# A fused attention and feed-forward kernel: states transposed by one DMA, a bank for the second G1, copies spread over two engines, and a G2 step moved

## The chip, the cores and the metric

The kernel runs on one core of one Trainium2 chip. The metric is the device time of one execution in microseconds (us). A "run" is one execution; medians over runs are given. The profile is one execution taken by the hardware profiler; its span (first to last instruction) is about 1.8 us shorter than the time of the same execution.

Engines are named as the profile names them: PE is TensorE's matmuls, PEld its weight loads, DVE is VectorE, ACT is ScalarE, POOL is GpSimd, SP is SyncE (here the queue that issues stores and DMA transposes). PSUM is the memory that matmuls write to, used here as eight banks; SBUF is the memory that holds their operands. A table load is the instruction with which ACT changes from exp to SILU or back; it takes 1.28 us in these traces.

## The reference

```python
# x: (8, 8, 512, 64), state: (8, 8, 32, 64); B, H, S, D and 32 state rows
a     = softmax(x @ state^T / 8);  xread = a  @ state      # 512 rows per batch
a2    = softmax(state @ x^T / 8);  sread = a2 @ x          # 32 rows per batch
t     = concat(xread, sread) over rows, heads side by side # (4352, 512)
h     = t @ w_in                                           # 512 -> 2048
out   = (h * sigmoid(h)) @ w_out                           # 2048 -> 512
```

The kernel never forms xread. For each batch it multiplies the states into w_in first (it calls the product W), so that h is the normalised a times W.

## The kernel before

Words used below:

- **G1 k** is one step of the first big product: 128 of the 2048 hidden columns, all 512 tokens of a batch. It is two matmuls of 512 columns into one PSUM bank, followed by one SILU on ACT that writes `g`. Steps 0 to 15 belong to batch 0, 16 to 31 to batch 1.
- **G2(b, tt, ft)** is one matmul of the second product: 128 tokens (tt), hidden block ft, summed over 16 blocks in one bank.
- **aT** is the normalised a, transposed so that G1 can read it.
- **W matmuls** are groups of eight small matmuls that form a piece of W, which DVE or ACT then copies to SBUF.

The pool that G1 writes to (`psH`) has two banks, so G1 k+2 has to wait for the SILU of G1 k. All eight PSUM banks are in use: `psO` has two (o0, o1), `psH` two (h1), `psA` four (a0 to a3).

```python
def g1_first():                                   # G1 0, in two halves, two banks
    ...
    for hg in range(2):
        for i in range(2):
            nc.tensor.matmul(pss[i][:, 0:256], W1[0][:, hg, 0:128], aT[0][:, hg, ds(2*i, 2), :],
                             start=(hg == 0), stop=(hg == 1), ...)
    for i in range(2):
        nc.scalar.activation(g[:, ds(256*i, 256)], pss[i][:, 0:256], func=SILU, bias=0.0)

def g1_half(k, hg):
    if hg == 0:
        h_ps[k] = psH.tile([128, 512], FP32, tag="h1", name="h1")
    ...

def G2(b, tt, ft):
    if ft == 0:
        if b == 0 and tt >= 2:
            outs[tt] = psA.tile([128, DM], FP32, tag=f"a{tt - 2}", name="o_a")   # tt 3 uses a1
    ...

# --- start, batch 0
pe_transpose_x(0, 1, 2, new_h, (nc.vector, nc.vector))
...
norm(0, 1, ((nc.vector, 0, 4),))
pss0 = w1_mms(0, [(0, 128)])
nc.scalar.activation(warm[:], busy[:, 0:1], func=SILU, bias=0.0)   # table load for SILU
w1_out(0, [(0, 128)], (nc.scalar, nc.scalar), pss0)
...
pe_transpose_a(0, 0, nc.scalar, new_o)
for c in (0, 2):
    pe_transpose_a(0, 1, nc.vector, (new_o, bank)[c // 2], c, 2)
upto(1)                                                            # G1 0
w1_out(0, [(128, 128)], (nc.vector, nc.vector), pss0)
w1_out(0, [(128, 256)], both, pss0, 128)

# --- end of batch 0 (G2 of the last 128 tokens), G1 of batch 1 begins
for ft in range(F3, NFT):
    ...
    if ft == 14:
        ...
        pss1 = w1_mms(1, cols, tail_bank)
        w1_out(1, cols, both, pss1)          # both = (DVE, ACT)
        ...
        transpose_x(2)                       # DMA transpose on SP
    if ft == 15:
        upto(NFT + 2)                        # G1 16, G1 17
    G2(0, 3, ft)
upto(NFT + 3)                                # G1 18
store(0, 3, nc.vector)

# --- batch 1
            if tt == 0:
                upto(NFT * b + min(lead + ft, NFT))        # lead is 4 for batch 1
            if b == 1:
                if at == (0, 1):
                    transpose_x(3)
                    transpose_state()        # eight PE transposes into a bank
                    for u in range(2):
                        evict_state(u, nc.vector)
```

The softmax here doesn't subtract the row's maximum and nothing guards it: scores larger than these inputs give would overflow.

## Time and profile before

| | before |
|---|---|
| time, median of the 3 runs known at the prediction | 217.85 us (217.42 to 218.06) |
| profiled run | 217.45 us, span 215.7 us |
| PE busy | 208.4 us, 97% of the span |

The page of the kernel before, its first lines (engine, busy us, share of the span, instructions):

```profile
span 215.7 us, 3904 instructions
PE 208.4 (97%) x1583; PEld 97.1 (45%) x1583; DVE 75.6 (35%) x167; ACT 140.2 (65%) x245; POOL 39.5 (18%) x61
```

PE is busy nearly all the time, so the time changes only when a PE instruction or a PE gap goes away. The list of waits of PE in the same kernel, cut (who waited for whom: us in total, times, longest):

```profile
PE ps_w L463 <- DVE W L158: 0.7, 1, 0.7
PE h L516 <- ACT g L510: 0.4, 1, 0.4
...
PE h L516 <- ACT g L548: 0.3, 1, 0.3
```

The list has only waits that leave the pipeline idle for over 0.15 us. Smaller losses are found by stepping through the starts. A 512-column matmul in an unbroken row starts 0.216 us after the one before. The Trainium skill ("TensorE: Matmul & The Clock Gate", section "Wait — 56ns, not 53.3ns?") states 215.7 ns for this, and the trace agrees. Every start that comes later than that is a loss, and "wait" below means the excess over 0.216 us.

The start in the timeline of PE, kernel before (start us, us, engine, line, operation, out<-in, shape, count, and in brackets the idle time and who ended it). L501 is G1 0, L516 the other G1, L557 a G2:

```profile
11.65 0.60 PE L501 MATMUL h<-aT,W 128*128 128x256 bf16 x4
12.61 0.59 PE L516 MATMUL h<-aT,W 128*128 128x512 bf16 x2 [0.36 <-ACT g L510]
13.04 0.59 PE L557 MATMUL o<-w_out_sb,g 128*128 128x512 bf16 x2
13.47 0.59 PE L557 MATMUL o_a<-w_out_sb,g 128*128 128x512 bf16 x2
```

G1 1 starts 0.96 us after G1 0 began. It waits for the first SILU of G1 0, because it takes that SILU's bank.

The place where batch 1 begins, PE and then ACT, kernel before (L463 are W matmuls, L278 the state transposes):

```profile
37.98 0.62 PE L463 MATMUL ps_w<-w_in_sb,stT 64*32 64x512 bf16 x16
38.54 0.39 PE L557 MATMUL o_a<-w_out_sb,g 128*128 128x512 bf16 x1
38.76 1.03 PE L516 MATMUL h<-aT,W 128*128 128x512 bf16 x4
39.63 0.38 PE L557 MATMUL o_a<-w_out_sb,g 128*128 128x512 bf16 x1
40.11 1.08 PE L516 MATMUL h<-aT,W 128*128 128x512 bf16 x4
41.03 0.38 PE L557 MATMUL o<-w_out_sb,g 128*128 128x512 bf16 x1
41.39 0.59 PE L516 MATMUL h<-aT,W 128*128 128x512 bf16 x2
41.82 0.61 PE L278 MATMUL ps_st<-ident,st_b 128*128 128x128 bf16 x8
42.27 0.38 PE L557 MATMUL o<-w_out_sb,g 128*128 128x512 bf16 x1
```

```profile
38.49 1.08 ACT L156 ACTIVATE W<-ps_w 128x512 bf16<-128x512 f32 x2 [0.77 <-PE ps_w L463]
39.46 1.09 ACT L548 ACTIVATE g<-h 128x512 bf16<-128x512 f32 x2
```

The G2 at 39.63 should be followed 0.216 us later by G1 18, but G1 18 starts at 40.11: a wait of 0.27 us. It waits for the SILU of G1 16. That SILU starts only at 39.46, because ACT copies two pieces of W first. Two smaller waits follow, 0.06 us before G1 19 and 0.14 us before G1 20. The eight state transposes hold PE from 41.82 to 42.27.

### The profile page before, as it was taken

The numbers are of one execution on the slowest core, as the hardware profiler recorded it, in microseconds if no ns is written. First come the engines' busy times: TensorE is split into PE (matmuls) and PEld (weight loads), VectorE is DVE, ScalarE is ACT, GpSimd is POOL, SyncE is SP. The second block draws the span as 40 slices with busy tenths as digits, with TensorE's granted clock in tenths as the row PEclk, the third lists the DMA queues.
The fourth block names the chain that finished last, engine by engine and source line by source line (L and its number), as shares of the span: only waits on it lengthen the run. The fifth ranks groups of instructions, "written<-read, shape, count | busy, mean of one in ns | idle before, by whom it ended". The sixth has DMA issues, their size and how long they took to land.

```text
span 215.7 us, 3904 instructions
## 1 busy us (share of the span) xinstructions
PE 208.4 (97%) x1583; PEld 97.1 (45%) x1583; DVE 75.6 (35%) x167; ACT 140.2 (65%) x245; POOL 39.5 (18%) x61
## 2 busy tenths in 40 slices
PE   7889999999899999999999999999999999999993
PEld 2443345445344444444444444444444444466653
DVE  3724237654961056106610552135411415200011
ACT  3766578699656985699559957786665366634410
POOL 8583013701520122004010402000200000000000
PEclk9999999999999999999999999999999999999999
DMA  6999999792339567273637194114310211011112
GB/s 197 195 204 206 294 273 331 194 272 101 77 95 256 176 105 195 62 233 96 157 97 232 68 184 112 49 49 106 86 59 6 101 49 52 0 50 49 52 49 97
DMA packets 41858, 28.40 MB, mean 132 GB/s; under 512 B 26992, under 2 KB 36720, under 8 KB 41840
## 3 DMA queue, kind: packets, MB, share of 16 engines
q1 hardware_dynamic: 35664, 20.39, 34.6%
q0 software_dynamic: 5888, 7.64, 17.1%
q8 instruction: 12, 0.20, 0.4%
q10 hardware_dynamic: 288, 0.13, 0.2%
q14 instruction: 6, 0.05, 0.1%
HBM read 17.43 MB, written 8.91 MB: 122 GB/s over the span
## 4 chain that ended last, share of the span: by engine, by line
PE 86%; DVE 5%; ACT 4%; DMA 2%; issue 1%; POOL 0%; POOLq 0%
PE o L557 46%; PE h L516 25%; PE ps_w L463 4%; PE h L537 3%; DMA x_f<-in_x_dram 2%; PE o_a L557 2%; PE o_part L579 2%; DVE W L158 2%; DVE rs L379 1%; ACT exp_nat L320 1%; PE ps_sr L415 1%; DVE rc L431 1%; PE ps_xt L251 1%; ACT g L548 1%; ACT W L156 1%
## 5 line engine op out<-in xcount | busy, mean ns | idle before, releaser
L557 PE MATMUL o<-w_out_sb,g 128*128 128x512 bf16 x496 | 132.2, 379 | 0.0
L548 ACT ACTIVATE g<-h 128x512 bf16<-128x512 f32 (+1 forms) x143 | 81.5, 573 | 35.8 <-PE h L516 21.8
L557 PEld LDWEIGHTS <-g 128*128 128x128 bf16 x528 | 50.0, 98 | 58.0 <-issue 3.6
L516 PE MATMUL h<-aT,W 128*128 128x512 bf16 x254 | 74.8, 379 | 0.8 <-ACT g L510 0.4
L158 DVE COPY o_sb<-o 128x512 f32<-128x512 f32 x15 | 10.4, 691 | 90.2 <-PE o L557 85.5
L516 PEld LDWEIGHTS <-W 128*128 128x128 bf16 x254 | 24.6, 98 | 31.7 <-DVE W L158 2.0
L158 DVE CAST W<-ps_w 128x512 bf16<-128x512 f32 (+2 forms) x34 | 21.5, 653 | 25.8 <-PE ps_w L463 25.8
L156 ACT ACTIVATE W<-ps_w 128x512 bf16<-128x512 f32 (+2 forms) x34 | 17.9, 567 | 13.3 <-PE ps_w L463 13.3
L158 POOL CAST x_nat<-x_f 128x512 bf16<-128x512 f32 x24 | 14.6, 653 | 33.2 <-DMA x_f<-in_x_dram 22.2
L156 ACT ACTIVATE o_sb<-o 128x512 f32<-128x512 f32 x16 | 9.6, 597 | 12.1 <-PE o L557 8.9
L362 POOL TENSOR_TENSOR an<-e,rcn 128x512 bf16<-128x512 bf16 x5 | 7.6, 1518 | 49.5 <-DVE rcn L360 49.5
L463 PE MATMUL ps_w<-w_in_sb,stT 64*32 64x512 bf16 (+2 forms) x264 | 11.1, 375 | 0.7 <-DVE W L158 0.7
L557 PE MATMUL o_a<-w_out_sb,g 128*128 128x512 bf16 x32 | 10.2, 379 | 0.0
L537 PE MATMUL h<-xmT,w_in_sb 128*128 128x256 bf16 x64 | 9.6, 273 | 0.0
L537 PEld LDWEIGHTS <-w_in_sb 128*128 128x128 bf16 x64 | 6.3, 98 | 3.9
L164 PE MATMUL ps_busy<-busy 128*128 128x512 bf16 x16 | 6.0, 491 | 1.2 <-DVE warm L171 1.2
L463 PEld LDWEIGHTS <-stT 64*32 64x32 bf16 x264 | 3.4, 89 | 7.3 <-issue 4.9
L382 POOL TENSOR_TENSOR an<-exp_nat,rc 128x512 bf16<-128x512 bf16 x3 | 3.1, 1050 | 19.2 <-ACT eT L346 11.4
L749 ACT ACT_TABLE_LOAD x5 | 6.4, 1283 | 0.1
L346 ACT ACTIVATE eT<-ps_scT 128x512 bf16<-128x512 f32 x10 | 5.4, 595 | 1.6 <-PE ps_scT L332 1.6
L359 DVE TENSOR_REDUCE rs<-e 128x32 f32<-128x1024 bf16 x5 | 6.0, 1208 | 0.0
L108 POOL DMA_DIRECT2D x_f<-in_x_dram x4 | 3.3, 842 | 12.1 <-DVE x_rows L158 10.0
(76 smaller groups left out, 105.1 us busy)
## 6 DMA issues: line engine op xcount, KB each, us to landing
out_dram<-o_sb SPq DMA_DIRECT2D x33, 256.0 KB, 2.4
x_f<-in_x_dram SPq DMA_DIRECT2D x4, 1024.0 KB, 6.2
x_f<-in_x_dram POOLq DMA_DIRECT2D x2, 1024.0 KB, 12.6
w_in_sb<-in_moe_w_in_dram POOLq DMA_DIRECT2D x3, 512.0 KB, 9.6
w_out_sb<-in_moe_w_out_dram POOLq DMA_DIRECT2D x3, 512.0 KB, 11.3
x_f<-in_x_dram SPq DMA_DIRECT2D x2, 512.0 KB, 4.7
x_f<-in_x_dram POOLq DMA_DIRECT2D x2, 512.0 KB, 14.3
w_out_sb<-in_moe_w_out_dram POOLq DMA_DIRECT2D x2, 256.0 KB, 7.7
```

The costliest lines, as they stand in the source:

```text
L156: nc.scalar.activation(dst, src, func=COPY, bias=0.0)
L158: eng.tensor_copy(dst, src)
L164: nc.tensor.matmul(ps[:], busy[:, 0:128], busy[:], start=True, stop=True, skip_group_check=True)
L346: nc.scalar.activation(t[:, hg], scT_ps[hg][:], func=EXP, bias=0.0, scale=SCALE)
L359: nc.vector.tensor_reduce(rs[:], e2[b][:], axis=AX, op=ADD)
L362: eng.tensor_tensor(a[:, hg], e2[b][:, hg], rc[:, hg].to_broadcast([128, 4, 4, NS]), op=MULT)
L463: nc.tensor.matmul(pss[f, hg][ds(32 * s, 32), 0:n], stT[ds(r, 64), b, h // 2, s % 2, :], w_in_sb[ds(r, 64), h // 2, ds(f, n)], start=True, ...
L516: nc.tensor.matmul(h_ps[k][:], W1[b][:, hg, ds(128 * ft, 128)], aT[b][:, hg, :, :], start=(hg == 0), stop=(hg == 1), skip_group_check=True,)
L537: nc.tensor.matmul(ps[:, 0:256], w_in_sb[:, kt, ds(128 * ft, 128)], xmT[:, :, kt].rearrange("p t n b -> p t (n b)"), start=(kt == 0), stop ...
L548: nc.scalar.activation(g[:, 0:n], ps[:, 0:n], func=SILU, bias=0.0)
L557: nc.tensor.matmul(outs[tt][:], gt[b * NFT + ft][:, ds(128 * tt, 128)], w_out_sb[:, ft, :], start=(ft == 0), stop=(ft == NFT - 1), skip_gr ...
L749: nc.scalar.activation(warm[:], busy[:, 0:1], func=SILU, bias=0.0)
```

## The change

Its intent: shorten the start, take the state transposes off PE, and remove the waits where batch 1 begins. The diff, complete except for the definition lines that are cut as marked:

```diff
-    st_ps = []
-    def transpose_state():
-        ps = bank([128, 8, B, 4, 2, 2], BF16, "ps_st")
-        ... eight nc.tensor.transpose(..., st_b[:, m, :], ident[:])
+    st_x = pers.tile([128, 8, B, 4, 2, 2], BF16)
+    def transpose_states():
+        nc.sync.dma_start_transpose(
+            st_x.rearrange("q m b k u n -> q m (b k u n)"), st_b.rearrange("p m w -> p (m w)")
+        )
@@ evict_state
-                    st_ps[0][
+                    st_x[
@@ g1_first
-        for hg in range(2):
-            for i in range(2):
+        for i in range(2):
+            for hg in range(2):
@@ g1_half
-            h_ps[k] = psH.tile([128, 512], FP32, tag="h1", name="h1")
+            pool, tag = (psA, "a1") if k == 1 else (psH, "h1")
+            h_ps[k] = pool.tile([128, 512], FP32, tag=tag, name="h1")
@@ start
-    pe_transpose_x(0, 1, 2, new_h, (nc.vector, nc.vector))
+    pe_transpose_x(0, 1, 2, new_h, (nc.vector, nc.scalar))
-    norm(0, 1, ((nc.vector, 0, 4),))
+    norm(0, 1, ((nc.vector, 0, 4),), 2)
-    pe_transpose_a(0, 0, nc.scalar, new_o)
     for c in (0, 2):
-        pe_transpose_a(0, 1, nc.vector, (new_o, bank)[c // 2], c, 2)
+        pe_transpose_a(0, 0, nc.scalar, new_o, c, 2)
+    for c in (0, 2):
+        pe_transpose_a(0, 1, nc.vector, bank, c, 2)
     upto(1)
     w1_out(0, [(128, 128)], (nc.vector, nc.vector), pss0)
-    w1_out(0, [(128, 256)], both, pss0, 128)
+    w1_out(0, [(128, 256)], (nc.vector, nc.vector), pss0, 128)
+    upto(2)
@@ end of batch 0
-            w1_out(1, cols, both, pss1)
+            w1_out(1, cols, (nc.vector, nc.vector), pss1)
             ...
+            transpose_states()
             transpose_x(2)
-        if ft == 15:
             upto(NFT + 2)
         G2(0, 3, ft)
@@ batch 1
                         transpose_x(3)
-                        transpose_state()
+                    if at == (0, 4):
                         for u in range(2):
                             evict_state(u, nc.vector)
-                    if at == (0, 4):
                         spread_x(2)
```

Called "the start part" below: everything in `g1_first`, `g1_half` and "start". Called "the batch 1 part": the rest.

More of the change, by code (lines that the diff above doesn't have):

```diff
@@ L270 @@
     pe_transpose_x(0, 0, 2, new_o, (nc.vector, nc.vector))
-    st_ps = []
-    def transpose_state():
-        ps = bank([128, 8, B, 4, 2, 2], BF16, "ps_st")
-        st_ps.append(ps)
-        for m in range(8):
-            nc.tensor.transpose(
-                ps[:, m].rearrange("p b k u n -> p (b k u n)"), st_b[:, m, :], ident[:]
-            )
+    st_x = pers.tile([128, 8, B, 4, 2, 2], BF16)
[3 more added lines that the diff above has]
+        )
     def evict_state(u, eng):
```

## The prediction

> **What bounds the kernel now.** TensorE. The profile page gives PE busy 208.4 us of a 215.7 us span (97%), clock granted in full. From start to start a 512-column matmul takes 0.216 us in the timeline; the Trainium skill ("TensorE: Matmul & The Clock Gate", "Wait — 56ns, not 53.3ns?") states 215.7 ns warm, so the trace agrees. Only a TensorE instruction or gap removed can count. From 62 us on the timeline has almost no longer step (45 to 93 ns each). The gaps lie in the start, in batch 0, and where batch 1 begins.
>
> **Start (to 13.9 us).** The chain of waits runs x load, exp, a 1.28 us table load, ACT W copies, ACT copy of aT (to 11.60), first G1 (11.65), SILU (12.17), then G1 of step 1 at 12.605, held by the SILU for its bank: 0.52 us more than the natural step. The change
> - splits the ACT aT copy: its first half (estimate 0.39 us, as another 256-column ACT copy) is ready at 11.43 instead of 11.60; the first SILU then needs two matmuls instead of three: it starts at 11.9 instead of 12.17;
> - gives G1 of step 1 its own bank: it starts at about 12.0, held by its DVE copies of W instead of the SILU, and the first G2 starts at about 12.45 instead of 13.035;
> - but that bank (a1) is the one that the fourth G2 accumulates in, so this G2 waits for the SILU of step 1 (0.60 us, ending near 13.2). I expect it at 13.26, against 13.68.
>
> Net gain at the second G1/G2 step: 0.42 us. The ACT copy of x and the split reduction gain nothing, since ACT's chain ends last.
>
> Batch 0 keeps it if the weights are there: each load lands 1.1 us or more before its use (second w_in block lands 14.6, used 15.72; third 20.0, used 21.34), though the queue is saturated there and won't move. Its gaps (0.2 to 0.4 us at 21.3, 22.6, 28.1, 29.4) are tied to PE's own progress and shift along.
>
> **Start of batch 1 (37.9 to 42.5 us).** Eight state transposes on PE (41.820 to 42.266): 0.446 us removed. In their place one DMA transpose on the SP queue: 8 blocks; the e<-eT transposes of the same size take 1.3 us of the queue and 3.1 us to land, so it lands near 42.5 and the DVE copies end near 45.5. First need: the batch 2 scores at 49.4. The x transposes behind it are delayed 1.3 us, with over 2 us to spare. Off the path.
> The gaps at 40.11 (0.27), 40.60 (0.06) and 41.39 (0.14 us) come from ACT evicting W (2 x 0.54 us) ahead of the SILUs. With W all on DVE and a G2 (0.216 us) between G1 17 and G1 18 they shrink to about 0.03 + 0.14. Gain about 0.28 us.
> Together 0.73 us; the 0.68 us wait at 58.94 (DVE chain of batch 1) stays.
>
> **Predicted.** 217.85 - 0.42 - 0.73 = 216.7 us; 8 in 10 between 216.2 and 217.4. Faster by over 2%: 1%; within 2%: 98%; slower: 1%.
>
> **Right if** the after trace shows: G1 step 1 starting within 0.4 us of the first G1's end; a short wait before the fourth G2; no state transposes on PE; G1 18 without a wait; the second G2 step of batch 1 (42.27 before) near 41.1; everything behind shifted by the same 1.1 us.
>
> **Wrong if** halves of a tile are not tracked apart (start gain only 0.2); DVE, with four W copies and the state copies, becomes late for a G1 or the scores; the DMA transpose lands after about 46 us; or a weight load lands later and absorbs the start's gain.

## The result, and the profile after

| | before | after |
|---|---|---|
| time, median of 4 runs | 217.64 us (217.42 to 218.06) | 216.30 us (216.27 to 216.76) |
| ratio | | 0.9941 (95% interval 0.9919 to 0.9963) |
| profiled run | 217.45 us, span 215.7 us | 216.30 us, span 214.5 us |

A ratio is the mean time of one kernel's fast runs over that of the other's of the same rounds, so it is not quite the ratio of the medians quoted beside it.

The page and the list of PE's waits (cut likewise), kernel after:

```profile
span 214.5 us, 3893 instructions
PE 208.0 (97%) x1575; PEld 96.8 (45%) x1575; DVE 76.7 (36%) x170; ACT 139.5 (65%) x244; POOL 39.4 (18%) x61
```

```profile
PE ps_w L460 <- DVE W L158: 0.7, 1, 0.7
...
PE h L514 <- ACT g L546: 0.3, 1, 0.3
PE ps_at L396 <- ACT W L156: 0.2, 1, 0.2
```

Eight matmuls are gone, the wait for the SILU of G1 0 is gone, the 0.7 us wait of batch 1 stayed, and a new wait is there: a transpose of a (`ps_at`) waits for ACT's copy of W. The same code has other line numbers than before (L514 was L516, L555 was L557, L460 was L463, L498 was L501).

The start in PE's timeline, kernel after:

```profile
11.41 0.70 PE L498 MATMUL h<-aT,W 128*128 128x256 bf16 x4
12.03 0.60 PE L514 MATMUL h<-aT,W 128*128 128x512 bf16 x2
12.47 0.59 PE L555 MATMUL o<-w_out_sb,g 128*128 128x512 bf16 x2
12.90 0.79 PE L555 MATMUL o_a<-w_out_sb,g 128*128 128x512 bf16 x2
13.53 0.59 PE L514 MATMUL h<-aT,W 128*128 128x512 bf16 x2
```

G1 1 now follows G1 0 by 0.61 us instead of 0.96. The two `o_a` matmuls take 0.79 us together instead of 0.59: the second, at 13.318, waits 0.20 us. It writes bank a1, which the SILU of G1 1 reads until 13.267.

The place where batch 1 begins, PE and then ACT, kernel after:

```profile
38.16 1.04 PE L514 MATMUL h<-aT,W 128*128 128x512 bf16 x4
39.04 0.59 PE L555 MATMUL o_a<-w_out_sb,g 128*128 128x512 bf16 x2
39.47 1.07 PE L514 MATMUL h<-aT,W 128*128 128x512 bf16 x4
40.37 0.38 PE L555 MATMUL o<-w_out_sb,g 128*128 128x512 bf16 x1
40.75 0.59 PE L514 MATMUL h<-aT,W 128*128 128x512 bf16 x2
41.18 0.38 PE L555 MATMUL o<-w_out_sb,g 128*128 128x512 bf16 x1
```

```profile
38.81 1.08 ACT L546 ACTIVATE g<-h 128x512 bf16<-128x512 f32 x2 [1.46 <-PE h L514]
40.10 1.08 ACT L546 ACTIVATE g<-h 128x512 bf16<-128x512 f32 x2 [0.21 <-PE h L514]
```

The SILU of G1 16 starts 0.64 us after G1 16 now (before: 0.70), but G1 18 comes one G2 later in PE's order, and it starts at 39.47 without a wait. Waits of 0.04 us (before G1 19) and 0.16 us (before G1 20) remain. The G2 that stood at 42.27 stands at 41.18.

What became of the states is in the view of the new tile, kernel after:

```profile
L158 DVE COPY stT<-st_x x8: 320/324/335, 42.5 to 44.9; 64x192 bf16<-64x192 bf16 x8
L275 SPq DMA_TRANSPOSE st_x<-st_b x1: 1402/1402/1402, 39.1 to 39.1; - x1
...
DMA to landing us min/median/max: 3.3/3.3/3.3
```

The DMA transpose occupies the SP queue for 1.40 us and lands 3.3 us after its issue, at 42.45. The copies end at 45.19 and the first matmul that needs them starts at 48.30. The x transposes behind it landed at 44.49 and 47.25 (before 43.45 and 46.21), the first of them also needed at 48.30.

### Where the time went, by stretches

Single executions differ at the start (see the experiments), so the trace was cut at four marks on PE and ACT and the stretches compared. T is the start of ACT's table load ahead of the first SILU. The first W mark is the first W matmul of batch 0's column 512, near 15.7 us. The column-score mark is the first matmul of batch 3's scores, near 52 us, in which states are the rows (`ps_scT`). The numbers are starts in the traces, in us:

| kernel | T | T to first W | first W to column scores | column scores to end |
|---|---|---|---|---|
| before | 9.207 | 6.510 | 36.390 | 163.573 |
| after | 9.260 | 6.091 | 35.669 | 163.500 |
| difference | +0.053 | -0.419 | -0.721 | -0.073 |

The sum is -1.16 us, the difference of the two spans. The stretches, not the spans, are compared below.

T itself comes 0.053 us later after the change. The last copy of the transposed x ended at 8.420 us on DVE before; it ends at 8.475 on ACT now, and the scores behind it start at 8.531 instead of 8.478. e_bound, with the start of before, has T at 9.210; the four runs below with the new start, no late x load and the first transposes not cold throughout have it at 9.264 to 9.274.

The last 0.073 us lie wholly behind PE's work: from the column scores to the last matmul all starts, counted from that mark, agree within 0.01 us in the two traces, and from the start of the last matmul to the end of the span it takes 3.526 us after and 3.600 before.

### The profile page after: what moved, and what is told of

The parts are those of the page before. It is cut to its first block, busy times and chain, and to the rows that moved or that the text cites. A ratio compares the mean times of both kernels' runs of the same rounds, so it can differ in the third digit from the quotient of the medians.

```text
span 214.5 us, 3893 instructions
## 1 busy us (share of the span) xinstructions
PE 208.0 (97%) x1575; PEld 96.8 (45%) x1575; DVE 76.7 (36%) x170; ACT 139.5 (65%) x244; POOL 39.4 (18%) x61
## 4 chain that ended last, share of the span: by engine, by line
PE 87%; DVE 4%; POOL 3%; ACT 3%; issue 1%; POOLq 0%
PE o L555 47%; PE h L514 26%; PE ps_w L460 4%; PE h L535 3%; PE o_a L555 2%; PE o_part L577 2%; DVE W L158 1%; POOL w_in_sb L149 1%; POOL w_out_sb L152 1%; ACT exp_nat L317 1%; DVE rs L376 1%; PE ps_sr L412 1%; DVE rc L428 1%; PE ps_xt L251 1%; PE ps_scT L329 1%
## 5 line engine op out<-in xcount | busy, mean ns | idle before, releaser
L555 PE MATMUL o<-w_out_sb,g 128*128 128x512 bf16 x496 | 132.2, 379 | 0.0
L555 PEld LDWEIGHTS <-g 128*128 128x128 bf16 x528 | 50.0, 98 | 57.6 <-issue 3.2
L514 PE MATMUL h<-aT,W 128*128 128x512 bf16 x254 | 74.8, 379 | 0.4 <-ACT g L546 0.3
L514 PEld LDWEIGHTS <-W 128*128 128x128 bf16 x254 | 24.5, 98 | 31.8 <-issue 2.0
L158 DVE CAST W<-ps_w 128x512 bf16<-128x512 f32 (+2 forms) x37 | 23.0, 649 | 25.3 <-PE ps_w L460 25.3
L156 ACT ACTIVATE W<-ps_w 128x512 bf16<-128x512 f32 (+1 forms) x31 | 16.4, 570 | 12.6 <-PE ps_w L460 12.6
L460 PE MATMUL ps_w<-w_in_sb,stT 64*32 64x512 bf16 (+2 forms) x264 | 11.1, 375 | 0.7 <-DVE W L158 0.7
L555 PE MATMUL o_a<-w_out_sb,g 128*128 128x512 bf16 x32 | 10.2, 379 | 0.0
L460 PEld LDWEIGHTS <-stT 64*32 64x32 bf16 x264 | 3.4, 89 | 7.3 <-issue 4.9
L748 ACT ACT_TABLE_LOAD x5 | 6.4, 1283 | 0.1
```

The costliest lines, as they stand in the source:

```text
L156: nc.scalar.activation(dst, src, func=COPY, bias=0.0)
L158: eng.tensor_copy(dst, src)
L460: nc.tensor.matmul(pss[f, hg][ds(32 * s, 32), 0:n], stT[ds(r, 64), b, h // 2, s % 2, :], w_in_sb[ds(r, 64), h // 2, ds(f, n)], start=True, ...
L514: nc.tensor.matmul(h_ps[k][:], W1[b][:, hg, ds(128 * ft, 128)], aT[b][:, hg, :, :], start=(hg == 0), stop=(hg == 1), skip_group_check=True,)
L555: nc.tensor.matmul(outs[tt][:], gt[b * NFT + ft][:, ds(128 * tt, 128)], w_out_sb[:, ft, :], start=(ft == 0), stop=(ft == NFT - 1), skip_gr ...
```

## The experiments

Twelve kernels ran, in three groups; each group had its own runs of the kernel before. All gave correct results. Theory A is the prediction's: each part of the change removes a piece of PE's time, the start part about 0.4 us and the batch 1 part about 0.73 us, and the two add up. Rivals were: B, batch 0 is paced by its weight loads and swallows the start's gain; C, only the removed transposes count.

| run | T | T to first W | first W to column scores | column scores to end | median us | ratio to before (95%) |
|---|---|---|---|---|---|---|
| e_start | 9.423 | 6.088 | 36.389 | 163.547 | 217.26 | 0.9983 (0.9970 to 0.9995) |
| e_bound | 9.210 | 6.510 | 35.670 | 163.487 | 216.79 | 0.9965 (0.9952 to 0.9977) |
| e_pe_states | 9.741 | 6.089 | 36.119 | 163.558 | 216.87 | 0.9969 (0.9957 to 0.9982) |
| e_bank_h | 9.264 | 6.223 | 35.996 | 163.499 | 216.43 | 0.9947 (0.9933 to 0.9961) |
| e_w_both | 9.269 | 6.088 | 35.932 | 163.471 | 216.56 | 0.9952 (0.9940 to 0.9965) |
| e_g2_back | 9.267 | 6.092 | 35.873 | 163.495 | 216.54 | 0.9950 (0.9936 to 0.9964) |
| e_g1_ahead | 9.482 | 5.892 | 35.676 | 163.482 | 216.11 | 0.9938 (0.9923 to 0.9953) |
| e_chunk_late | 9.274 | 6.093 | 35.676 | 162.615 | 215.45 | 0.9900 (0.9887 to 0.9912) |
| after_again | 9.421 | 6.089 | 35.674 | 163.501 | 216.32 | 0.9944 (0.9931 to 0.9958) |
| e_best | 9.425 | 5.891 | 35.673 | 162.622 | 215.34 | 0.9901 (0.9888 to 0.9915) |
| e_best_lead | 9.424 | 5.891 | 35.477 | 162.824 | 215.39 | 0.9899 (0.9885 to 0.9912) |
| e_best_at | 9.418 | 5.760 | 35.476 | 162.820 | 215.23 | 0.9896 (0.9883 to 0.9910) |

The medians of before in the three groups were 217.59, 217.62 and 217.58 us. In the traces of the second and third group some matmul records are missing (242 or 243 of 254 G1 matmuls found), which does not touch the marks.

### e_start: the start part alone

Edit: the kernel before with the hunks `g1_first`, `g1_half` and "start" of the change, nothing else.

> The kernel before with the start part of the change alone (order of the first G1, own bank for G1 step 1, x and aT copies split over two engines, W copies on DVE). Theory A (the start gain is real and is carried through batch 0, as every weight load lands over 0.8 us before its use): G1 of step 2 starts near 13.53 us instead of 13.90, no wait for a load afterwards, the gaps of batch 0 keep their sizes, profiled span 215.3 us, time 0.36 us under before (ratio 0.998). Theory B (batch 0 is paced by its saturated weight loads, so the start gain is swallowed there, and the whole gain of the change comes from the start of batch 1): G1 of step 2 is early as well, but gaps between 15 and 33 us grow by about 0.36 us together, span 215.7 us, ratio 1.000.

Measured: T to first W shrank by 0.42 us, and from there to the column scores it took 36.389 us, against 36.390 before. The gaps of batch 0 kept their sizes to 0.01 us, so nothing was swallowed and B falls. The span was 215.4 us, 0.1 above the expectation, and G1 2 stood at 13.69 instead of 13.53. That lies before T, which came 0.16 us later than in after. The reason is in the timeline of PE near 5.4 us: the eight first transposes of x, in this run and then in the kernel after:

```profile
5.47 1.06 PE L251 MATMUL ps_xt<-ident,x_rows 128*128 128x128 bf16 x8
```

```profile
5.37 0.62 PE L251 MATMUL ps_xt<-ident,x_rows 128*128 128x128 bf16 x8
```

Their starts are 0.106 us apart here and 0.056 us there. The Trainium skill ("TensorE: Matmul & The Clock Gate", "Wait — 56ns, not 53.3ns?") gives 106.7 ns for a cold clock and 55.6 ns for a warm one at 128 columns, and says in "What's actually happening" that the window after which the clock is released runs freely and does not reset when a kernel starts. The trace agrees with both figures; that this is the clock is inferred from the spacing, since the granted clock that the profile gives for this stretch is 1.00 in both runs. No run here shows the window. The same code ran cold in after_again and warm in after, so a difference of up to 0.2 us at the start belongs to the execution and not to the kernel. All six executions in which these eight transposes ran cold throughout have T at 9.42 to 9.48 us.

### e_bound: the batch 1 part alone

Edit: the kernel before with the other hunks of the change.

> The kernel before with the batch 1 part alone (states by one DMA transpose, all four last W copies of batch 1 on DVE, the G2 step moved between G1 17 and G1 18). Theory A: the second G2 step of batch 1 comes 0.73 us earlier, near 41.5 us (0.45 from the transposes, 0.28 from smaller gaps at G1 18 to 20), span 214.95 us, ratio 0.9967. Theory B: it must carry the whole change, 1.1 us, span 214.6 us. Theory C (only removed TensorE work counts, the moved copies and the moved G2 do nothing): 0.45 us, span 215.25 us.

Measured: first W to column scores 35.670 us, 0.720 less than before; T to first W unchanged (6.510). A said 0.73, B 1.1, C 0.45. A stands; C falls. The two parts together, 0.42 and 0.72, give the two stretches of the change exactly.

### e_pe_states: the states back on PE

Edit, on the kernel after: `transpose_state()` and its place of before, the DMA transpose removed; everything else stays.

> The changed kernel with the states transposed by TensorE again. Theory A: the eight transposes come back as 0.446 us of TensorE and nothing else moves, span 214.95 us, second G2 step of batch 1 at about 41.63 us instead of 41.18. If the DMA transpose has a hidden price (it delays the two x transposes behind it on the queue by about 1.2 us), the x transposes land 1.2 us earlier here and the loss is smaller than 0.45 us, span under 214.8 us.

Measured: first W to column scores 36.119 us, 0.450 more than after: the 0.446 us of the transposes and nothing else. The DMA transpose has no hidden price here. The expected span was missed (215.5 instead of 214.95 us): in the profiled execution, the slowest of the five at 217.29 us, the first x load landed at 5.31 us instead of 4.86, and T came 0.48 us late. The last stretch was 0.06 us longer as well, as in the other two kernels with PE transposes. This lies behind PE's work too: from the start of the last matmul to the end it takes 3.573 to 3.600 us in these three and 3.502 to 3.526 in the eleven others. Why is not known.

### e_bank_h: what the own bank is worth

Edit, on the kernel after:

```diff
-            pool, tag = (psA, "a1") if k == 1 else (psH, "h1")
-            h_ps[k] = pool.tile([128, 512], FP32, tag=tag, name="h1")
+            h_ps[k] = psH.tile([128, 512], FP32, tag="h1", name="h1")
```

> The changed kernel with G1 of step 1 in its old pair of banks again. Theory A: G1 step 1 waits for the first SILU and starts at 12.36 us instead of 12.03, but the wait of 0.20 us before the fourth G2 vanishes, so the net loss is only about 0.12 us: G1 step 2 at 13.65 us instead of 13.53, span 214.65 us. Rival: the own bank is worth the whole wait that it removes, 0.33 us or more: G1 step 2 at 13.86 us, span 214.9 us.

Measured: T to first W 6.223 us, 0.132 more than after. The timeline of PE in this run:

```profile
11.42 0.70 PE L498 MATMUL h<-aT,W 128*128 128x256 bf16 x4
12.37 0.59 PE L513 MATMUL h<-aT,W 128*128 128x512 bf16 x2 [0.25 <-ACT g L507]
...
13.23 0.59 PE L554 MATMUL o_a<-w_out_sb,g 128*128 128x512 bf16 x2
```

G1 1 waits for the SILU again (12.37 instead of 12.03), but the fourth G2 no longer does (the two `o_a` take 0.59 us together). The own bank removes a wait of 0.34 us and gives 0.20 us of it back. The rival (worth 0.33 us or more) falls. The other 0.29 us of the start's gain remain here: the first SILU starts 2.675 us after T, as in after, against 2.963 before. No run takes apart what brings that SILU forward (the order of G1 0, the split copies of aT, the reduction in two parts).

This trace has one surprise, in its list of PE's waits:

```profile
PE o L554 <- DMA w_out_sb<-in_moe_w_out_dram: 0.2, 1, 0.2
```

In this execution the second half megabyte of w_out landed at 18.57 us (17.10 in before, 17.39 in after), and G2 step 4 stood still for 0.33 us; that is why the next stretch is 35.996 and not 35.67 us. The profiled run was the slowest of its five (216.75 us; two others were 216.41). So batch 0 can be paced by a load in a single execution. Nothing shows that the change makes this more frequent.

### e_w_both and e_g2_back: the copies and the moved G2, each taken out alone

Edits, on the kernel after; first e_w_both, then e_g2_back:

```diff
-            w1_out(1, cols, (nc.vector, nc.vector), pss1)
+            w1_out(1, cols, both, pss1)
```

```diff
-            upto(NFT + 2)
+        if ft == 15:
+            upto(NFT + 2)
         G2(0, 3, ft)
```

> The changed kernel with the last four W copies of batch 1 shared between VectorE and ScalarE again (the G2 step stays moved). Theory A (the W copies on ScalarE stand in front of the two first SILUs and hold G1 18 to 20 through their bank): counted between the start of G1 step 2 and the start of G1 21, the stretch grows by about 0.21 us against the 27.86 us of the changed kernel (waits 0.25 + 0.09 + 0.07 us at G1 18, 19 and 20 instead of 0 + 0.04 + 0.16). Rival (the moved G2 alone covers the SILU, the engine of the copies does not matter): the stretch stays within 0.05 us of 27.86.

> The changed kernel with the G2 step back in its old place (after the W matmuls, ahead of G1 16; W copies all on VectorE). Theory A (the moved G2 fills the time in which G1 18 would wait for the SILU of G1 16): the stretch from G1 step 2 to G1 21 grows by about 0.14 us (waits 0.17 + 0.07 + 0.10 us at G1 18, 19, 20). Rival (with ScalarE free of copies the place of the G2 does not matter): within 0.05 us of 27.86 us.

Measured in the stretch from first W to column scores: e_w_both 0.263 us more than after (expected 0.21), e_g2_back 0.204 more (expected 0.14). Both rivals fall. The single waits, in us:

| | before G1 18 | before G1 19 | before G1 20 | sum |
|---|---|---|---|---|
| before (copies shared, G2 not moved) | 0.27 | 0.06 | 0.14 | 0.47 |
| e_w_both (copies shared, G2 moved) | 0.27 | 0.06 | 0.14 | 0.47 |
| e_g2_back (copies on DVE, G2 not moved) | 0.20 | 0.06 | 0.14 | 0.40 |
| after (copies on DVE, G2 moved) | 0.00 | 0.04 | 0.16 | 0.20 |

The two edits do not add. Moving the G2 alone gains nothing, moving the copies alone gains 0.07 us, both together 0.27 us. ACT's timeline in e_w_both shows why:

```profile
38.12 1.09 ACT L156 ACTIVATE W<-ps_w 128x512 bf16<-128x512 f32 x2 [0.76 <-PE ps_w L460]
39.09 1.09 ACT L546 ACTIVATE g<-h 128x512 bf16<-128x512 f32 x2
```

With copies on ACT, the SILU of G1 16 starts when the copies end, however early G1 16 was issued, and G1 18 follows that SILU; a reordering on PE cannot help. With copies on DVE, the SILU follows G1 16 itself, and only then does it matter that G1 16 is issued one G2 earlier and G1 18 no earlier than before.

### e_g1_ahead: removing the wait that the own bank brought

Edit, on the kernel after:

```diff
         for tt in range(4 if ft < F3 else 3):
+            if (ft, tt) == (0, 3):
+                upto(3)
             G2(0, tt, ft)
```

> The changed kernel with G1 step 2 issued ahead of the fourth G2 of step 0, whose bank the SILU of step 1 still reads. If the wait of 0.20 us before that G2 is a price of the own bank that only the order sets, it vanishes and everything behind comes 0.20 us earlier: from the SILU table load (start 9.26 us) to the first G1 of step 3 9.26 -> 0.20 us less, span about 214.3 us. If another engine (the W copies on VectorE, or the SILU of step 1 itself through the other banks) holds the following G1, the gain is under 0.05 us.

Measured: T to first W 5.892 us, 0.199 less than after. The wait before the fourth G2 was a matter of order alone: G1 2 fills it. The span stayed at 214.5 us, because this profiled execution ran the start cold (T at 9.482, the x transposes 0.107 us apart). The median is 216.11 us against 216.30; one of the six runs was 217.16.

### e_chunk_late: the wait that both kernels have

Edit, on the kernel after:

```diff
-                    if at == (2, 8):
+                    if at == (2, 12 if b == 1 else 8):
                         w1_chunks(n, (2, 3), both)
```

> The changed kernel with the W matmuls of columns 1024 to 2047 for batch 2 four G2 steps (0.86 us) later in batch 1. Both kernels wait 0.68 us there (at 58.94 us before, 57.85 after) for a bank that VectorE empties late. If that wait is a chain of a fixed length (last SILU, table load, exp, reductions, sread copies, W copy), later matmuls find the bank free: the wait vanishes, 0.68 us less, span about 213.85 us, ratio to before about 0.991. If the wait moves along with the matmuls (VectorE still busy with what follows), the gain is under 0.2 us.

Measured: column scores to end 162.615 us, 0.885 less than after, with a median of 215.45 us. The wait vanished, so the chain that it waits for does not move along with the matmuls. PE's timeline there, kernel after and then e_chunk_late:

```profile
56.77 0.41 PE L460 MATMUL ps_w<-w_in_sb,stT 64*32 64x512 bf16 x8
57.85 0.41 PE L460 MATMUL ps_w<-w_in_sb,stT 64*32 64x512 bf16 x8 [0.68 <-DVE W L158]
```

```profile
57.65 0.63 PE L460 MATMUL ps_w<-w_in_sb,stT 64*32 64x512 bf16 x16
```

The gain is larger than the 0.68 us that the profile shows as idle. The idle time is counted from the end of the matmuls before. From start to start, the second group comes 1.08 us after the first when it waits and 0.23 us after it when it does not: 0.85 us.

### after_again, e_best, e_best_lead, e_best_at: better kernels

after_again is the kernel after, unchanged. e_best has the edits of e_g1_ahead and e_chunk_late. e_best_lead has these, with

```diff
-        lead = 4 if b == 1 else 6
+        lead = 3 if b == 1 else 6
-                    if at == (2, 8):
+                    if at == (2, 14 if b == 1 else 8):
```

e_best_at adds to e_best_lead that the first transposed a goes to one bank and is copied in halves (the definition of `pe_transpose_a`, which gets a parameter for this, is cut), and that the third piece takes the bank that this frees:

```diff
-    for c in (0, 2):
-        pe_transpose_a(0, 0, nc.scalar, new_o, c, 2)
+    pe_transpose_a(0, 0, nc.scalar, new_o, 0, 4, 2)      # one bank, two copies
     for c in (0, 2):
-        pe_transpose_a(0, 1, nc.vector, bank, c, 2)
+        pe_transpose_a(0, 1, nc.vector, (new_o, bank)[c // 2], c, 2)
```

> The changed kernel itself once more, beside the three below on the same chip: 216.3 us, ratio to before 0.994. From the table load ahead of the first SILU to G1 step 2 it takes 4.27 us (before 4.69), from G1 step 2 to the first scores matmul of batch 3's column form (the ps_scT group) 37.49 us (before 38.21); theory A needs both numbers again, whatever the start does.

> The changed kernel with both additions that paid by themselves: G1 step 2 ahead of the fourth G2 (0.20 us) and the W matmuls of batch 2 four G2 steps later (0.86 us measured alone). They lie in different stages, so they add up: 1.05 us under the changed kernel, about 215.25 us, ratio to before 0.989. If the late W chain only just fitted, the earlier start leaves it as it was, since chain and matmuls shift together.

> As e_best, with batch 1 started on a lead of three G1 steps instead of four, and the late W matmuls two G2 steps later still. The waits of 0.04 and 0.16 us before G1 19 and G1 20 should vanish, because a G2 now stands between each two G1s: 0.20 us less than e_best, about 215.05 us. If the chain behind the last G1 (which comes one G2 step later here) reaches another bank or the scores late, the 0.20 us is lost again and the time equals that of e_best.

> As e_best_lead, with the first transposed a in one bank, copied in two halves, so that the third transposed piece gets a free bank and not the one that ScalarE still copies W from (the changed kernel's TensorE waits 0.2 us for that, near 10.97 us). First G1's second matmul starts about 0.1 us earlier after the table load; the first SILU too. Since G1 step 1 then still waits for VectorE's W copies, the net gain is 0.07 us at most, under what the times can tell; the stretch from the table load to the first G2 (3.21 us in the changed kernel) should shrink to about 3.14 us.

Measured:

- after_again repeats every stretch of after to 0.005 us, except T, 0.16 us later with a cold start. The stretches carry the comparison, the start does not.
- e_best adds up as expected: 0.20 and 0.88 us in their stretches, median 215.34 us against 216.32 of after_again.
- e_best_lead is a miss with a lesson. The waits before G1 19 and G1 20 vanished (35.477 instead of 35.673 us, 0.20 less), and the next stretch took 0.20 us more. The time is that of e_best. The profile of e_best_lead and then that of e_best, from their timelines (W matmuls, the exp of batch 2 on ACT, and the first matmuls of sread, cut off where the window ends):

```profile
50.40 1.08 ACT L317 ACTIVATE exp_nat<-ps_sc 128x512 bf16<-128x512 f32 x2
...
51.02 0.92 PE L460 MATMUL ps_w<-w_in_sb,stT 64*32 64x512 bf16 x16
...
51.87 0.31 PE L412 MATMUL ps_sr<-x_rows,exp_nat 128*32 128x65 bf16 x16
```

```profile
50.38 1.09 ACT L317 ACTIVATE exp_nat<-ps_sc 128x512 bf16<-128x512 f32 x2
51.22 0.71 PE L460 MATMUL ps_w<-w_in_sb,stT 64*32 64x512 bf16 x16
51.85 0.34 PE L412 MATMUL ps_sr<-x_rows,exp_nat 128*32 128x65 bf16 x20
```

  The two exps end at 51.48 and 51.47 us in the two kernels: they follow the last G1 of batch 1, which stands where it stood, because one more G2 now lies before it. PE reaches the W matmuls 0.2 us earlier, and the second half of them, whose bank the second exp still reads (by the order in which the program takes its banks), resumes after that exp (its next weight load is at 51.54). The gain turned into a new wait 10 us later.
- e_best_at: T to the first G2 3.077 us, against 3.207 in e_best_lead, and T to first W 0.131 us less. The expectation was 0.07 at most. The step that was mis-sized: it took DVE's W copies as fixed, but DVE starts them after its two copies of a, and those came earlier too (the first W copy starts at 11.657 us, against 11.852 in e_best_lead). The median, 215.23 us, is the lowest, 1.09 us under after_again; against e_best the difference is within the spread of the runs, and the stretches decide.

## Why the prediction was right or wrong

The prediction was 216.7 us, range 216.2 to 217.4; measured 216.30 us. Taken step by step:

- **"What bounds the kernel" (PE)**: right. All that was gained shows as starts of PE instructions, but for 0.07 us behind the last matmul.
- **Start, 0.42 us**: right in the mechanisms. Counted from T the gain is 0.419 us, but T came 0.053 us later, so that the second G1/G2 step gained 0.37 us by the clock of the trace. The prediction said that ACT's copy of x gains nothing; it did not see that it costs this. The three mechanisms are there: the first SILU starts at 11.94 (said 11.9), G1 1 at 12.03 (said 12.0), the fourth G2 waits and starts at 13.32 (said 13.26). e_bank_h and e_g1_ahead confirm the wait and its price.
- **What it did not see at the start**: the transposed a of the second head group (the kernel handles the eight heads in two groups of four) moved from a free bank to one from which ACT still copies W. PE waits for that (0.2 us in the list of waits), and e_best_at shows that it costs 0.13 us. Nor does ACT's chain end last here, as the prediction said: the second matmul of G1 0 (11.629) follows DVE's copy of aT, which ends at 11.576, while ACT's first half is ready at 11.363. So the reduction in two parts, which was said to gain nothing, probably gains: a of the second head group is ready 1.45 us after T with it and 1.85 before, and at the old pace it would come at 11.11 (an estimate: 9.260 + 1.846), behind the 10.974 at which its transpose starts. No run tests this alone.
- **Batch 0 carries the gain**: right, by e_start; with the exception of one execution with a late load. The room is smaller than the prediction's 1.1 us, though: the load of the second w_in block, said to land at 14.6, landed at 14.89 in after, 0.46 us before its use, and in e_best_at 0.26 us before it. Over the fourteen traces it landed between 14.45 and 15.07, so a still shorter start may find this load in its way.
- **State transposes, 0.446 us, off the path**: right, by e_pe_states (0.450 us).
- **Waits at G1 18 to 20, 0.28 us**: right in size (0.27). The prediction took copies and G2 as one; the experiments show that neither is worth much without the other.
- **Time**: the predicted difference, 1.15 us, is the difference of the two profiled runs (217.45 to 216.30). The prediction is 0.4 us too high. About half of that is its base: it took its 1.15 us from the median of three runs, 217.85, and later medians of the same kernel lie at 217.58 to 217.64. Against those the gain is 1.26 to 1.34 us, so the change was under-predicted by 0.1 to 0.2 us. The sum fits the two profiled runs partly by luck: the stretches give 1.14 us, the later T takes 0.05 us of it, and the 0.07 us behind the last matmul, which the prediction did not have, give about as much back. The rest of the difference of the medians is not explained; single executions differ by more than it at the start (cold or warm, late loads).

## What to carry to other kernels

Where two kinds of work share an engine ahead of a consumer (here copies and SILUs on ACT, ahead of G1 18), look which one ends last before reordering the consumer's engine: here the reordering gained nothing until the copies were gone. Test such pairs both ways, because the gains need not be a sum. A borrowed PSUM bank is free only until its next owner arrives: look up who writes it next, and fill that time with other work. And when gains are a few tenths of a microsecond, compare stretches between marks in the trace rather than spans, and look for the place where an earlier engine merely arrives sooner at the next fixed chain.

## What the Trainium skill lacked or had wrong

- "ScalarE: Activation LUTs", "What ACT_TABLE_LOAD costs": the load itself is as stated (1.283 us in the traces, 1283 ns on the page). The drain of about 1380 ns that the page adds to every switch does not appear here: in after the load starts 19 ns after the exp before it ended (9.241 to 9.260), and the next activation starts 11 ns after the load's end (10.543 to 10.554).
- "TensorE: Matmul & The Clock Gate", "Part 4: PE-mode transpose", gives 390 ns alone and 275 ns in a kernel for a 128x128 transpose, and no cost in a row. Here one takes 0.219 us by itself (L205 in before) but eight in a row hold PE for 0.446 us, 0.056 us each, and removing them gained 0.450 us.
- No page that was found says that the idle time that a profile gives before a waiting matmul can be less than what the wait costs: 0.68 us shown, 0.85 us from start to start.
